# Delta-rule attention with two MLPs on one core: head-major operands, compact keys in 64x64 blocks, Newton roots, new order weights

## The chip, the cores and the metric

The kernel runs on one core of a Trainium2 chip. A core has TensorE (PE in the profile, its weight loads as PEld), VectorE (DVE), ScalarE (ACT), GpSimd (POOL) and SyncE (SP), which issues all of this kernel's DMAs; 16 DMA engines move the data. The metric is the device time of one execution in microseconds (us); less is better.

## The reference

Attention with the delta rule over 4 batches, 8 heads, 768 tokens and heads of 48, and then two gated MLPs over the 384 columns that the heads make together.

```python
k_n = k / (norm(k) + 1e-06)
for t in range(S):                       # per batch and head; state is 48x48
    y[:, :, t] = q[:, :, t] @ state
    v_old = state @ k_n[t]
    state = state + b[t] * outer(k_n[t], v[t] - v_old)
# first MLP: gate = sigmoid(causal convolution of x over 5 tokens)
x = (gate * (x @ w_val)) @ w_out
# second MLP: h = gelu(x @ w_in), halves u and v; v_n = layer norm of v
v_s = w_sg @ v_n + b_sg                  # mixes all 768 tokens of a batch
out = x + (u * v_s) @ w_out2
```

## The kernel before

**Precision.** Nearly every product is made of three float16 matmuls: an operand is split into a high and a low half, and high*high, high*low and low*high are summed (`mm3`, and `mmh` for four heads at a time). So nearly every operand is written twice: ScalarE writes the high half, VectorE or GpSimd the low one (`hl_psum`, `hl_sbuf`).

**Attention.** The 768 tokens of a batch are cut into 12 chunks of 64, 48 chunks in all (`NSEQ`). The 8 heads stand as two halves of 4: the first four in partitions 0 to 63, the others in 64 to 127, and a stationary operand is a block diagonal 128x128 matrix with zeros off the diagonal blocks, so that one matmul serves two heads. Chunks go in pairs (`d`, 24 of them), and four pairs make a set (`k`, 6 of them).

For a set, `norm(k)` loads the keys and makes reciprocal norms, with the helper `rsqrt`. For a pair, `keys(d)` scales the keys (`kf`), splits them into the block diagonal `kp` (for the first two pairs straight into `kj`), transposes them with matmuls against an identity (`pk<-i,kp`), copies the result into `kst` and lets DMAs spread it into the block diagonal; the prepared pair goes to DRAM (`keys_d`). `gram(d)` multiplies keys with keys (`pk<-kst,kp`) and takes the diagonal 32x32 blocks out into `gd` and the others into `gx`. `base(k)` inverts a set's 32x32 triangles on VectorE: 30 pairs of dependent operations (`tmp<-X` and `X<-X,tmp`) with transposes around them. `merge(d)` joins two 32-token inverses into one of 64 (`m1p`, `tbd`). `seq(n)` carries the state through the chunks: `ps_q<-wh,kj`, `rh`, `ps_q<-rh,tbd`, `wh`, `ps_state<-wh,kj`, `wh` again, each waiting for the one ahead of it. `attend(n)` makes the chunk's output from `ws`, a block diagonal copy of `wh` made by DMA, and from `qh` and `mh`. `fetch(d)` brings a prepared pair back from `keys_d` into one of two `kj` buffers.

**MLPs.** For 256 tokens at a time: `front` (convolution on VectorE, `a<-x,cw,a`), `value`, `hidden` (with a layer norm, which uses `rsqrt` on two columns), `gates`, `mix` and `final`. `mix` needs `hidden` of all of its batch's tokens, so that the last batch's mixing stands behind the last chunk of attention.

**Layout.** The attention's float16 operands have the head as their innermost index: a stationary operand of one head is read with a step of 4 elements, and so is the moving operand `wh`.

**Order.** No loop sets the order. Every call is recorded as an `Op` (all instructions therefore carry the helper's line, L106), and `in_order` plays the program through with estimated costs: on each engine the ready operation with the longest remaining chain goes next. The length of a chain is a sum over its operations, weighted per engine by the table `CHAIN` (a weight on an operation's time and a charge for going over to another engine). Each engine then runs its list strictly in this order.

Of the kernel before, what the change touches and what calls it, by code (L numbers as in the profile page):

```python
# [236 lines left out]
CHAIN = dict(tensor=(0.65, 0.064), scalar=(0.756, 0.047), vector=(2.464, 0.104), gpsimd=(0.748, 0.014), sync=(2.315, 0.036))  # L237
# [88 lines left out]
def kernel(  # L326
# [19 lines left out]
    C = 64  # L346
# [14 lines left out]
    NK, NTB, NWS, LA = 2, 2, 3, 5  # L361
# [30 lines left out]
    mhalf = const.tile([P, 1], F32, name="mhalf")  # L392
    nc.gpsimd.memset(mhalf, -0.5)
# [11 lines left out]
    def bdt(nm, i):  # L405
        if (nm, i) not in bd:
            t = const.tile([P, 4, 128, PR] if nm == "ws" else [P, 2, U, 128], F16, name=f"{nm}{i}")
            clear(nc.gpsimd, t)
            bd[nm, i] = t
        return bd[nm, i]  # L410


    kj, kprep = {}, []

    def kbd_of(keys):
        return keys[:, 0:4]

    def ktb_of(keys):
        return keys[0:EP, 4:8].rearrange("p (x i) f h -> p x i f h", x=2)
# [4 lines left out]
    for t in kj[0], kj[1], *kprep:  # L424
        clear(nc.vector, t[:, 0:4])
        clear(nc.gpsimd, t[:, 4:8])
# [94 lines left out]
    def keys(d):  # L521
# [4 lines left out]
        direct, early = d < NK, d < SETD  # L526
        both = kj[d] if direct else kprep[d % NK]
        kbd, ktb = kbd_of(both), ktb_of(both)
        (nc.vector if early else nc.gpsimd).tensor_tensor(out=kf, in0=kf, in1=rs.unsqueeze(3).to_broadcast([P, 2, PR, E]),
                                                          op=ALU.mult)  # L530
# [103 lines left out]
    def fetch(d):  # L634
# [17 lines left out]
    def queries(n):  # L652
# [7 lines left out]
        for h in range(PR):  # L660
            mm3(pq[:, h, :], (ktb[:, 0, :, h], ktb[:, 1, :, h]), (qh[:, 0, h, :], qh[:, 1, h, :]), True, True)
# [10 lines left out]
    for i in range(NWS):  # L672
        whs.append(const.tile([P, 4, C, PR], F16, name=f"wh{i}"))
# [405 lines left out]
```

## Time and profile before

| | us |
|---|---|
| median of 3 runs (781.43 to 782.82) | 781.53 |
| the profiled execution | 775.91 |
| its span, first to last instruction | 773.6 |
| PE busy in the span (8088 matmuls) | 581.0 |
| DVE busy (1402 instructions) | 592.6 |
| ACT busy (958) | 492.8 |
| POOL busy (227) | 259.9 |

The span is what the rows further down divide up; 2.3 us lie around it. The profiled execution was 5.6 us faster than the median. A matmul's end is modelled in these rows, so the distance from one start to the next says more than its duration.

### The profile page before, as it was taken

Reading aid. Unit: us, or ns where it says so; the run is one execution under the profiler, and the core shown is the slowest. Engines: PE = TensorE matmul, PEld = TensorE weight load, DVE = VectorE, ACT = ScalarE, POOL = GpSimd, SP = SyncE. Lnnn points to the kernel's source line nnn. Section 1 sums busy time; section 2 is a strip of 40 time slices with the busy share of each in tenths; the row PEclk is TensorE's granted clock in tenths of the full one; section 3 lists DMA queues with packets and bytes.
Section 4 is the critical chain, followed back from the end, with each engine's and each line's share of the span. In section 5 each row is a group of like instructions: output and inputs, shape, how many; then the busy total and the mean of one; then the engine's idle time right before and its main releaser. Section 6 shows DMA issues by size and latency. Waiting matters only on the chain.

```text
span 773.6 us, 20377 instructions
## 1 busy us (share of the span) xinstructions
PE 581.0 (75%) x8088; PEld 490.3 (63%) x8088; DVE 592.6 (77%) x1402; ACT 492.8 (64%) x958; POOL 259.9 (34%) x227
## 2 busy tenths in 40 slices
PE   0433643665656666777979999999988999989897
PEld 0321333555556554556967897898785799876786
DVE  7887787987799989997778888999975875663222
ACT  5875773899589895879646699745463644534111
POOL 7646313526543474336260154200330400011100
PEclk9999985556755577989989999999999999999999
DMA  5451623588578856728638476486545182420121
GB/s 176 136 135 44 184 73 66 131 175 228 121 178 200 233 143 130 171 61 200 144 78 172 120 188 132 99 184 141 136 116 126 31 169 71 125 69 21 48 69 42
DMA packets 211183, 97.97 MB, mean 127 GB/s; under 512 B 83088, under 2 KB 203280, under 8 KB 211088
## 3 DMA queue, kind: packets, MB, share of 16 engines
q1 hardware_dynamic: 211088, 96.67, 52.0%
q8 instruction: 64, 1.05, 0.6%
q14 instruction: 31, 0.25, 0.1%
HBM read 51.81 MB, written 23.33 MB: 97 GB/s over the span
## 4 chain that ended last, share of the span: by engine, by line
PE 31%; DVE 20%; ACT 10%; DMA 5%; issue 4%; POOL 3%; SPq 1%; ACTq 0%; DVEq 0%; POOLq 0%
PE ps_mlp L106 23%; DVE a L106 5%; PE ps_y L106 3%; DVE X L106 2%; PE ps_q L106 2%; DMA m1p<-gx 2%; DMA kj<-keys_d 2%; DVE tmp L106 2%; POOL rs L106 1%; DVE wh L106 1%; DVE ps_mlp L106 1%; PE pk L106 1%; ACT v L106 1%; DVE rs_t L106 1%; ACT tbh L106 1%
## 5 line engine op out<-in xcount | busy, mean ns | idle before, releaser
L106 PEld LDWEIGHTS <-kj 112*128 112x128 f16 (+1 forms) x1712 | 121.4, 119 | 82.1 <-issue 51.0
L106 PE MATMUL ps_mlp<-wg,vnh 128*128 128x256 f16 x864 | 141.6, 276 | 5.6 <-ACT vnh L106 3.7
L106 PEld LDWEIGHTS <-kp 112*128 112x128 f16 (+1 forms) x880 | 65.1, 122 | 49.7 <-issue 28.1
L106 PEld LDWEIGHTS <-vnh 128*128 128x128 f16 x864 | 82.9, 100 | 14.0 <-ACT vnh L106 4.5
L106 DVE SCALAR_TENSOR_TENSOR a<-x,cw,a 128x256 f32<-128x256 f32 x144 | 82.3, 607 | 0.1
L106 PEld LDWEIGHTS <-ws 112*128 112x128 f16 (+1 forms) x1104 | 74.3, 119 | 10.0 <-issue 7.6
L106 PE MATMUL ps_mlp<-gth,w 128*128 128x256 f16 x432 | 79.9, 276 | 0.1
L106 PE MATMUL ps_mlp<-gvh,wi 128*128 128x256 f16 x432 | 77.6, 280 | 1.2 <-ACT o L106 0.5
L106 DVE TENSOR_TENSOR X<-X,tmp 128x30 f32<-128x30 f32 (+9 forms) x180 | 75.9, 422 | 1.5
L106 PEld LDWEIGHTS <-m1p 128*128 128x128 f16 x1152 | 62.2, 101 | 20.0 <-issue 11.0
L106 PE MATMUL ps_state<-wh,kj 128*128 128x48 f16 x528 | 55.1, 221 | 22.3 <-DVE wh L106 12.1
L106 DVE TENSOR_TENSOR tmp<-X 128x30 f32<-128x30 f32 (+9 forms) x180 | 69.6, 387 | 1.3
L106 PE MATMUL ps_q<-wh,kj 112*128 112x48 f16 x528 | 55.4, 219 | 20.0 <-DVE wh L106 12.3
L106 PE MATMUL ps_mlp<-wi,gvh 128*128 128x512 f16 x216 | 65.8, 405 | 5.5 <-DVE gvh L106 4.8
L106 POOL TENSOR_TENSOR kp<-kf,kp 64x384 f16<-64x384 f32 x42 | 47.0, 1120 | 55.2 <-ACT kp L106 44.3
L106 PE MATMUL ps_y<-mh,ws 128*128 128x64 f16 x576 | 63.5, 208 | 1.9 <-DVE mh L106 1.9
L106 PE MATMUL ps_y<-qh,ws 112*128 112x64 f16 x528 | 61.1, 208 | 4.1 <-DVE mh L106 4.0
L106 PE MATMUL pk<-kst,kp 112*128 112x64 f16 x504 | 51.5, 236 | 13.2 <-ACT kst L106 10.1
L106 PE MATMUL ps_mlp<-gvh,wo 128*128 128x256 f16 x324 | 56.8, 273 | 4.3 <-DVE gth L106 2.8
L106 ACT ACTIVATE kst<-pk 112x512 f16<-112x512 f32 x42 | 56.5, 1345 | 3.2 <-PE pk L106 2.6
L106 PE MATMUL ps_mlp<-xh,wv 128*128 128x256 f16 x324 | 51.8, 278 | 8.4 <-POOL xh L106 6.3
L106 PE MATMUL ps_q<-rh,tbd 128*128 128x48 f16 x576 | 42.8, 195 | 16.8 <-DVE rh L106 9.0
(147 smaller groups left out, 1544.6 us busy)
## 6 DMA issues: line engine op xcount, KB each, us to landing
keys_d<-kp SPq DMA_DIRECT2D x44, 256.0 KB, 4.2
ws<-wh SPq DMA_DIRECT2D x88, 128.0 KB, 3.6
kj<-keys_d SPq DMA_DIRECT2D x44, 256.0 KB, 4.9
wg<-wgd SPq DMA_DIRECT2D x12, 768.0 KB, 5.4
qf<-in_qt SPq DMA_DIRECT2D x24, 224.0 KB, 3.4
kf<-in_kn SPq DMA_DIRECT2D x12, 384.0 KB, 4.2
vf<-in_vn SPq DMA_DIRECT2D x24, 192.0 KB, 4.9
xd<-ys SPq DMA_DIRECT2D x48, 96.0 KB, 2.5
```

Source lines behind the costliest of these rows:

```text
L106: op.call()
```

## The change

1. `ws`, `kj` and `wh` become head-major: the head stands outside, and a head's 128 (or 64, or 48) columns lie next to each other. Stationary operands are then read with step 1, and so are `wh` and `kst` as moving operands; ScalarE and VectorE write them with step 1. A DMA into a block diagonal now writes runs of 64 elements (128 bytes) where it wrote 256 (512 bytes).
2. The two block diagonal buffers `kp` and the tile `kst` go; three compact buffers `kc` hold both the split keys and their transposes. The split is one ScalarE and one GpSimd instruction over 128 partitions in place of two of each over 64. The transposing and the key-by-key matmuls of each head half are single 64x64 blocks: 32 and 48 of them for a pair of chunks in place of 16 and 24. The DMAs from `kst` into `kp` go, and a prepared pair is stored by one DMA with 4 KB for a partition in place of two.
3. `gram` takes the diagonal blocks out by one ScalarE and one VectorE instruction with a mask (`which`) in place of four ScalarE instructions over 32 partitions.
4. `rsqrt` starts from a bit trick and makes three Newton steps, all on VectorE; GpSimd's power goes. That is 11 VectorE instructions in place of 3 (and one on GpSimd), for 6 norms and 12 layer norms.
5. The `CHAIN` weights are others, so that each engine's order changes throughout.

```diff
-CHAIN = dict(tensor=(0.65, 0.064), scalar=(0.756, 0.047), vector=(2.464, 0.104), gpsimd=(0.748, 0.014), sync=(2.315, 0.036))
+CHAIN = dict(tensor=(0.304, 0.758), scalar=(0.128, 0.167), vector=(2.092, 0.053), gpsimd=(0.876, 0.428), sync=(1.949, 0.262))
...
-        kj[d] = const.tile([P, 8, 128, PR], F16, name=f"kj{d}")
-        kprep.append(const.tile([P, 8, 128, PR], F16, name=f"kp{d}"))
+        kc.append(const.tile([P, 8, PR, C], F16, name=f"kc{d}"))
...
+        kj[d] = const.tile([P, 8, PR, 128], F16, name=f"kj{d}")
...
-        nc.gpsimd.tensor_tensor(out=y, in0=x, in1=mhalf.to_broadcast([P, n]), op=ALU.pow)
-        nc.vector.scalar_tensor_tensor(out=t, in0=y, scalar=-0.5, in1=y, op0=ALU.mult, op1=ALU.mult)
-        nc.vector.tensor_tensor(out=t, in0=t, in1=x, op=ALU.mult)
-        nc.vector.scalar_tensor_tensor(out=y, in0=t, scalar=1.5, in1=y, op0=ALU.add, op1=ALU.mult)
+        ti = t.bitcast(I32)
+        nc.vector.tensor_scalar(out=ti, in0=x.bitcast(I32), scalar1=1, scalar2=None, op0=ALU.logical_shift_right)
+        nc.vector.tensor_scalar(out=y.bitcast(I32), in0=ti, scalar1=-1.0, scalar2=float(0x5F3759DF),
+                                op0=ALU.mult, op1=ALU.add)
+        for _ in range(3):
+            nc.vector.scalar_tensor_tensor(out=t, in0=y, scalar=-0.5, in1=y, op0=ALU.mult, op1=ALU.mult)
+            nc.vector.tensor_tensor(out=t, in0=t, in1=x, op=ALU.mult)
+            nc.vector.scalar_tensor_tensor(out=y, in0=t, scalar=1.5, in1=y, op0=ALU.add, op1=ALU.mult)
...
-        for r in range(2):
-            eng = nc.vector if early and r == 0 else nc.gpsimd
-            rr, ff = slice(r * C, (r + 1) * C), slice(r * C, r * C + E)
-            hi, lo = (kbd[rr, 2 * x:2 * x + 2, ff].rearrange("p i e h -> p i h e") for x in range(2))
-            nc.scalar.activation(out=hi, in_=kf[rr], func=AF.Copy)
-            eng.tensor_tensor(out=lo, in0=kf[rr], in1=hi, op=ALU.subtract)
+        nc.scalar.activation(out=hi, in_=kf, func=AF.Copy)
+        eng.tensor_tensor(out=lo, in0=kf, in1=hi, op=ALU.subtract)
...
-                nc.tensor.matmul(out=pk[:, u, :], lhsT=kbd[:, 2 * x + u // PR, :, u % PR], rhs=i64, start=True, stop=True)
+                for r in range(2):
+                    rr = slice(r * C, (r + 1) * C)
+                    nc.tensor.matmul(out=pk[rr, u, :], lhsT=both[rr, 2 * x + u // PR, u % PR, :], rhs=i64[rr], start=True,
+                                     stop=True)
...
-        to_bd(ktb.rearrange("p x i t h -> p (x i) t h"), kst.rearrange("p x i t h -> p (x i) t h"), E)
-        for r in range(0 if direct else 2):
-            rr = slice(r * C, (r + 1) * C)
-            nc.sync.dma_start(out=keys_d[d, rr], in_=both[rr, :, rr].rearrange("p x t h -> p x (t h)"))
+        if d < NK:
+            to_bd(kj[d], both)
+        else:
+            nc.sync.dma_start(out=keys_d[d], in_=both.rearrange("p x h f -> p x (h f)"))
...
-            mm3(pg[:, u, :], (ktb[:, 0, i, :, h], ktb[:, 1, i, :, h]), (kst[:, 0, i, :, h], kst[:, 1, i, :, h]), True, True)
-        for r in range(4):
-            o = 32 * (r % 2)
-            dst, src = gd[32 * r:32 * r + 32, us, :], pg[32 * r:32 * r + 32, :, o:o + 32]
-            nc.scalar.activation(out=dst, in_=src, func=AF.Copy, scale=1.0 / (SK * SK))
+            for r in range(2):
+                rr = slice(r * C, (r + 1) * C)
+                k = (kst[rr, i, h, :], kst[rr, 2 + i, h, :])
+                mm3(pg[rr, u, :], k, k, True, True)
+
+        nc.scalar.activation(out=gd, in_=pg[:, :, 0:32], func=AF.Copy, scale=which[:, 0:1])
+        nc.vector.scalar_tensor_tensor(out=gd, in0=pg[:, :, 32:64], scalar=which[:, 1:2], in1=gd, op0=ALU.mult, op1=ALU.add)
...
-            nc.sync.dma_start(out=kj[d][rr, :, rr].rearrange("p x t h -> p x (t h)"), in_=keys_d[d, rr])
+            nc.sync.dma_start(out=kj[d][rr, :, :, rr], in_=keys_d[d, rr].rearrange("p x (h f) -> p x h f", h=PR))
```

Two places in the order matter further down. The first is VectorE's list at the third set's norm (`rs_t`, `rs` and `ss` belong to `rsqrt`; `tmp` and `X` to the second set's inversion). Before:

```order
L106 SCALAR_TENSOR_TENSOR wh_101<-ps_q,wh_101 128x4x48
L106 TENSOR_TENSOR X<-X,tmp 128x4x27
L106 SCALAR_TENSOR_TENSOR rs_t<-rs 128x32
L106 SCALAR_TENSOR_TENSOR gx<-pk,gx 128x256
L106 TENSOR_TENSOR tmp<-X 128x130
L106 TENSOR_TENSOR rs_t<-rs_t,ss 128x32
```

The first `rs_t` reads GpSimd's power, with the inversion's operations queued behind it. The same place of the changed kernel:

```order
L106 TENSOR_SCALAR rs_t<-ss 128x32
L106 TENSOR_TENSOR X<-X,tmp 128x3x28
L106 TENSOR_SCALAR rs<-rs_t 128x32
L106 TENSOR_TENSOR tmp<-X 128x108
L106 SCALAR_TENSOR_TENSOR rs_t<-rs 128x32
L106 TENSOR_TENSOR X<-X,tmp 128x4x27
L106 TENSOR_TENSOR rs_t<-rs_t,ss 128x32
L106 TENSOR_TENSOR tmp<-X 128x130
L106 SCALAR_TENSOR_TENSOR rs<-rs_t,rs 128x32
```

The root now stands on VectorE alone, one step between each two of the inversion. The second place is PE's list in the changed kernel near chunk 28, where a product of keys with keys (`pk<-kc`, 64x64) falls among work on operands of 128 rows, the MLP's and the attention's:

```order
L106 LDWEIGHTS gvh
L106 MATMUL ps_mlp<-wi,gvh 128x512
L106 LDWEIGHTS tbd_94
L106 MATMUL ps_q<-rh,tbd_94 128x48
L106 LDWEIGHTS kc_89
L106 MATMUL pk<-kc_89 64x64
L106 LDWEIGHTS ws_96
L106 MATMUL ps_y<-qh,ws_96 128x64
```

In the kernel before such work alternated too (here `pk<-kst,kp` between a matmul of the MLP and one of the state), but each took the array whole:

```order
L106 LDWEIGHTS wv
L106 MATMUL ps_mlp<-xh,wv 128x256
L106 LDWEIGHTS kp_91
L106 MATMUL pk<-kst,kp_91 128x64
L106 LDWEIGHTS kj_90
L106 MATMUL ps_state<-wh_102,kj_90 128x48
```

What moved is the shape: the interleaving was there, the switching between 64x64 and the whole array was not. In the changed list the 1920 blocks of 64x64 stand in 349 stretches, of which 266 are one block alone.

## Rows read from the trace of the kernel before

**Rows 1.** Stages: length, busy us (instructions) of each engine, granted clock, DMA share, GB/s.

```profile
0.00:48.00 48.00, 12.57 (x176) 10.66 (x176) 36.43 (x66) 34.04 (x64) 30.42 (x41) 1.00 0.54 162
48.00:123.00 75.00, 34.67 (x312) 20.07 (x313) 62.65 (x144) 50.51 (x91) 28.74 (x29) 0.92 0.36 93
123.00:344.00 221.00, 137.24 (x2351) 117.23 (x2351) 196.03 (x455) 173.87 (x328) 105.70 (x84) 0.67 0.68 159
344.00:663.00 319.00, 297.69 (x4386) 260.36 (x4384) 256.65 (x643) 202.76 (x417) 84.45 (x64) 0.98 0.58 132
663.00:773.00 110.00, 98.80 (x868) 81.98 (x866) 40.81 (x98) 31.65 (x59) 10.55 (x10) 1.00 0.18 53
```

**Rows 2.** Tile wh: count, ns min/median/max, first and last start.

```profile
L106 DVE SCALAR_TENSOR_TENSOR wh<-ps_q,wh x48: 559/592/628, 122.6 to 662.1; 128x192 f16<-128x192 f32 x48
```

**Rows 3.** Timeline, DVE: start us, us, instruction; a first and a twenty-first.

```profile
47.88 1.22 DVE L106 SCALAR_TENSOR_TENSOR gd<-gd,beta_sb 128x1024 f32<-128x1024 f32 x1
...
343.86 0.58 DVE L106 SCALAR_TENSOR_TENSOR wh<-ps_q,wh 128x192 f16<-128x192 f32 x1
```

**Rows 4.** Timeline at the third norm, DVE and POOL; brackets: idle before, releaser.

```profile
122.12 5.41 POOL L106 TENSOR_TENSOR rs<-ss,mhalf 128x32 f32<-128x32 f32 x1 [1.63 <-DVE ss L106]
122.56 0.57 DVE L106 SCALAR_TENSOR_TENSOR wh<-ps_q,wh 128x192 f16<-128x192 f32 x1
122.93 0.30 DVE L106 TENSOR_TENSOR X<-X,tmp 128x108 f32<-128x108 f32 x1
127.57 0.19 DVE L106 SCALAR_TENSOR_TENSOR rs_t<-rs 128x32 f32<-128x32 f32 x1 [4.34 <-POOL rs L106]
127.68 0.43 DVE L106 SCALAR_TENSOR_TENSOR gx<-pk,gx 128x256 f16<-128x256 f32 x1
```

**Rows 5.** Waits over the span: who for whom, us in total, times, longest.

```profile
DVE rs_t L106 <- POOL rs L106: 18.2, 6, 4.5
```

**Rows 6.** Groups by shape: count, busy us, mean ns of one, idle before.

```profile
L106 ACT ACTIVATE kst<-pk 112x512 f16<-112x512 f32 x42 | 56.5, 1345 | 3.2 <-PE pk L106 2.6
L106 ACT ACTIVATE kp<-kf 64x384 f16<-64x384 f32 x44 | 47.0, 1074 | 10.4 <-DMA keys_d<-kp 7.0 <-POOL kf L106 2.7
L106 POOL TENSOR_TENSOR kp<-kf,kp 64x384 f16<-64x384 f32 x42 | 47.0, 1120 | 55.2 <-ACT kp L106 44.3 <-issue 6.6 <-PE ps_q L106 2.3
L106 ACT ACTIVATE gd<-pk 32x256 f32<-32x256 f32 x88 | 33.0, 375 | 8.6 <-PE pk L106 7.7
L106 ACT ACTIVATE wh<-ps_q 128x192 f16<-128x192 f32 x48 | 29.5, 614 | 16.2 <-PE ps_q L106 14.6 <-PE ps_b L106 1.4
L106 DVE SCALAR_TENSOR_TENSOR wh<-ps_q,wh 128x192 f16<-128x192 f32 x48 | 28.5, 594 | 5.2 <-ACT wh L106 4.7
L106 DVE SCALAR_TENSOR_TENSOR rh<-ps_q,rh 128x192 f16<-128x192 f32 x44 | 15.3, 348 | 1.4 <-ACT rh L106 0.7
L106 ACT ACTIVATE rh<-ps_q 128x192 f16<-128x192 f32 x44 | 14.5, 328 | 12.6 <-DVE ps_q L106 12.2
L106 ACT ACTIVATE gth<-ps_mlp 128x512 f16<-128x512 f32 x24 | 14.3, 598 | 20.3 <-DVE ps_mlp L106 12.8 <-PE ps_mlp L106 5.3 <-PE ps_b L106 2.2
L106 DVE SCALAR_TENSOR_TENSOR gx<-pk,gx 128x256 f16<-128x256 f32 x22 | 9.2, 416 | 2.4 <-ACT gx L106 2.3
```

**Rows 7.** Timeline, a GpSimd operation beside one of VectorE's inversion.

```profile
118.96 0.22 DVE L106 TENSOR_TENSOR tmp<-X 128x84 f32<-128x84 f32 x1
...
119.58 0.91 POOL L106 TENSOR_TENSOR w<-wst,w 128x384 f16<-128x384 f32 x1 [16.61 <-ACT w L106]
119.67 0.92 DVE L106 TENSOR_TENSOR X<-X,tmp 128x84 f32<-128x84 f32 x1
```

**Rows 8.** Timeline, PE: matmuls in a row, first start to last end.

```profile
124.22 0.55 PE L106 MATMUL ps_q<-wh,kj 112*128 112x48 f16 x8 [0.46 <-ACT wh L106]
...
476.59 0.98 PE L106 MATMUL pk<-kst,kp 112*128 112x64 f16 x13
...
480.19 0.46 PE L106 MATMUL ps_q<-rh,tbd 128*128 128x48 f16 x12
```

**Rows 9.** Page, DMA queue: packets, MB, share of 16 engines.

```profile
q1 hardware_dynamic: 211088, 96.67, 52.0%
```

**Rows 10.** Tile kj: idle before its instructions, us and times, by releaser.

```profile
  DMA kj<-keys_d: 2.7, 3
```

More of the change, by code (lines that the diff above doesn't have):

```diff
@@ L359 @@
     EP = C + E
-    NK, NTB, NWS, LA = 2, 2, 3, 5
+    NK, NKC, NTB, NWS, LA = 2, 3, 2, 3, 5
     NGV, NVN, NV = NTT + 1, NT + 2, 3
@@ L406, in bdt @@
         if (nm, i) not in bd:
-            t = const.tile([P, 4, 128, PR] if nm == "ws" else [P, 2, U, 128], F16, name=f"{nm}{i}")
+            t = const.tile([P, 4, PR, 128] if nm == "ws" else [P, 2, U, 128], F16, name=f"{nm}{i}")
             clear(nc.gpsimd, t)
@@ L410, in bdt @@
         return bd[nm, i]
-    kj, kprep = {}, []
-    def kbd_of(keys):
-        return keys[:, 0:4]
+    kj, kc = {}, []
     def ktb_of(keys):
-        return keys[0:EP, 4:8].rearrange("p (x i) f h -> p x i f h", x=2)
+        return keys[0:EP, 4:8].rearrange("p (x i) h f -> p x i h f", x=2)
+    for d in range(NKC):
+        kc.append(const.tile([P, 8, PR, C], F16, name=f"kc{d}"))
+        clear(nc.vector, kc[d][:, 0:4])
     for d in range(NK):
-        kj[d] = const.tile([P, 8, 128, PR], F16, name=f"kj{d}")
-        kprep.append(const.tile([P, 8, 128, PR], F16, name=f"kp{d}"))
-    for t in kj[0], kj[1], *kprep:
-        clear(nc.vector, t[:, 0:4])
-        clear(nc.gpsimd, t[:, 4:8])
+        kj[d] = const.tile([P, 8, PR, 128], F16, name=f"kj{d}")
+        clear(nc.vector, kj[d][:, 0:4])
+        clear(nc.gpsimd, kj[d][:, 4:8])
     nc.gpsimd.memset(cmask, 1.0)
@@ L432 @@
     nc.sync.dma_start(out=beta_sb, in_=beta_in)
+    which = const.tile([P, 2], F32, name="which")
+    nc.gpsimd.memset(which, 0.0)
+    for r in range(4):
+        nc.gpsimd.memset(which[32 * r:32 * r + 32, r % 2:r % 2 + 1], 1.0 / (SK * SK))
     for nm, n in (("tbd", NTB), ("m1p", 1), ("ws", NWS)):
@@ L525, in keys @@
         kf, rs = sets["kf"][:, cs], sets["rs"][:, cs]
[L526 to L530, printed above, removed]
-        for r in range(2):
-            eng = nc.vector if early and r == 0 else nc.gpsimd
-            rr, ff = slice(r * C, (r + 1) * C), slice(r * C, r * C + E)
-            hi, lo = (kbd[rr, 2 * x:2 * x + 2, ff].rearrange("p i e h -> p i h e") for x in range(2))
-            nc.scalar.activation(out=hi, in_=kf[rr], func=AF.Copy)
-            eng.tensor_tensor(out=lo, in0=kf[rr], in1=hi, op=ALU.subtract)
-        kst = pp.tile([EP, 2, 2, C, PR], F16, name="kst", tag="kst", bufs=2)
+        early = d < SETD
+        both = kc[d % NKC]
+        hi, lo = (both[:, 2 * x:2 * x + 2, :, 0:E] for x in range(2))
+        eng = nc.vector if early else nc.gpsimd
+        eng.tensor_tensor(out=kf, in0=kf, in1=rs.unsqueeze(3).to_broadcast([P, 2, PR, E]), op=ALU.mult)
+        nc.scalar.activation(out=hi, in_=kf, func=AF.Copy)
+        eng.tensor_tensor(out=lo, in0=kf, in1=hi, op=ALU.subtract)
         for x in range(2):
@@ L540, in keys @@
             for u in range(U):
-                nc.tensor.matmul(out=pk[:, u, :], lhsT=kbd[:, 2 * x + u // PR, :, u % PR], rhs=i64, start=True, stop=True)
-            pk = pk[0:EP].rearrange("p (i h) t -> p i h t", h=PR)
-            kt = kst[:, x].rearrange("p i t h -> p i h t")
+                for r in range(2):
+                    rr = slice(r * C, (r + 1) * C)
+                    nc.tensor.matmul(out=pk[rr, u, :], lhsT=both[rr, 2 * x + u // PR, u % PR, :], rhs=i64[rr], start=True,
+                                     stop=True)
+            pk = pk.rearrange("p (i h) t -> p i h t", h=PR)
+            kt = both[:, 4 + 2 * x:6 + 2 * x]
             if early and x == 1:
@@ L547, in keys @@
                 nc.scalar.activation(out=kt, in_=pk, func=AF.Copy, scale=-1.0)
-        to_bd(ktb.rearrange("p x i t h -> p (x i) t h"), kst.rearrange("p x i t h -> p (x i) t h"), E)
-        for r in range(0 if direct else 2):
-            rr = slice(r * C, (r + 1) * C)
-            nc.sync.dma_start(out=keys_d[d, rr], in_=both[rr, :, rr].rearrange("p x t h -> p x (t h)"))
-        sets["kt", d] = (ktb, kst)
+        if d < NK:
+            to_bd(kj[d], both)
+        else:
+            nc.sync.dma_start(out=keys_d[d], in_=both.rearrange("p x h f -> p x (h f)"))
     def gram(d):
         us = slice(d % SETD * U, (d % SETD + 1) * U)
-        ktb, kst = sets.pop(("kt", d))
-        gd = sets["gd"]
+        kst = kc[d % NKC][:, 4:8]
+        gd = sets["gd"][:, us, :]
         pg = bank_of(d, 2)
@@ L672 @@
     for i in range(NWS):
-        whs.append(const.tile([P, 4, C, PR], F16, name=f"wh{i}"))
+        whs.append(const.tile([P, 4, PR, C], F16, name=f"wh{i}"))
         clear(nc.gpsimd, whs[i])
```

22 lines of the change are left out of this document (10 added, 12 removed).

## The prediction

> **What bounds the kernel now.** First the busy time by stage. Up to 344 us VectorE is the fullest engine, 295 of 344 us, ScalarE follows with 258, and PE has 184, at a granted clock of 0.67, so partly at 1.2 and partly at 2.4 GHz, from 123 to 344 us. From 344 to 663 us PE is busy for 298 of 319 us at 0.98, and from 663 us on for 99 of 110 [rows 1]. The reader is to see two kernels in one: VectorE, with ScalarE feeding it, sets the pace of the first half, PE that of the second. Next where the cuts lie: the first inversion starts at 47.9 us, chunk 0 has its `wh` at 123 us, chunk 20 at 344, chunk 47 at 663 [rows 2, 3]. The tail after that is MLP work that needs the last chunk, so its length stays, and the end moves by what the two halves move. Last the waits: VectorE, in the stage that it bounds, stands still for GpSimd's power (4.34 us at the third norm, the inversion queued behind) [rows 4], 18.2 us in six norms [rows 5].
>
> **Roots.** The power takes 5.41 us [rows 4], and `rs_t` waits at the head of VectorE's list. It goes, with a wait of 18.2/6, or 3.0 us, for each norm. Four of the six norms lie before 344 us: -12 us. In its place stand 8 more VectorE operations. Such an operation lasts 0.19 us and lets the next one start after 0.11 [rows 4]; the order puts them between the inversion's steps, so I take 0.11, with 0.19 as the other end. Four norms and, by 344 us, three layer norms have 7 x 8 = 56: +6 us (to +11).
>
> **Layout on VectorE and ScalarE.** `wh` is written with a step of 4 in 0.594 us on VectorE and 0.614 on ScalarE; `rh`, of the same size with step 1, takes 0.348 and 0.328 [rows 6]. By 344 us there are 41 writes of `wh` on each: 41 x 0.246 = -10 us for VectorE, 41 x 0.286 = -12 for ScalarE. `kst` takes 1.345 us, and `gth`, as large and with step 1, 0.598: 33 instances by then, -25 us on ScalarE. The split takes ScalarE 1.074 us twice for a pair of chunks; one instruction of 384 columns lies between `rh` (192 columns, 0.328) and `gth` (512, 0.598), say 0.5: for 20 pairs -33 us. GpSimd's 1.12 us twice becomes about 0.9 once [rows 6, 7].
>
> **Mask.** Four ScalarE instructions of 0.375 us become one; with a column of scales I put it at 0.5, for some 18 pairs -18 us. VectorE gets one more, priced by `gx` (0.416, same shape): 18 x 0.42 = +7.5 us [rows 6].
>
> **Sum to 344 us.** VectorE by itself: -12 + 6 - 10 + 7.5 = -8.5 us. ScalarE loses 88 of 258 us, a third. What that is worth is the unknown: VectorE is idle for 49 of the 344 us, 12 of them counted above, so between 0 and 37 us. I take a third, -12, since a third of ScalarE's work goes; the first inversion waits for `keys` and `gram` and starts earlier within this term. GpSimd's operations hold up VectorE's: beside a POOL operation of 0.91 us, 84 columns of the inversion took 0.92 in place of 0.22 [rows 7], 0.7 us for a hit. By 344 us GpSimd has some 18 fewer of these; if half hit, -6 (0 to -12). Together -26.5 us; with every term at its good end -57, at its bad end (Newton steps at 0.19 us, no relief) -3.5.
>
> **PE, 344 to 663 us.** Eight `ps_q<-wh,kj` in a row took 0.55 us, twelve `ps_q<-rh,tbd` 0.46 [rows 8]. Taking 0.2 us off for the last one's own length leaves 50 and 24 ns from start to start. Both move 48 columns; the first reads both operands with a step of 4, the second with step 1. Some 600 such matmuls lie in this stage (25 chunks with 24 each): at 22 ns each -13 us, and since PE is 93% busy, -12. The key products took 62 ns by the same working (13 in 0.98 us). About 250 of these and of the transpositions become 450 blocks of 64x64. No row shows one; between 24 and 62 ns apiece they come to 11 to 28 us, against some 13 now: -2 to +15. I take 0, near the lower end, because a step of 1 is what the 24 ns have in common with them. Switching between shapes is a rival below. ScalarE and VectorE also lose work here, but they aren't the bound.
>
> **DMA.** Two DMAs for each pair (`kst` into `kp`) go, and `gram` no longer waits for them; a stored pair is one DMA in place of two. Against that, `ws` and fetched keys are written in runs of 128 bytes: some 190,000 such pieces replace some 80,000 of 512. The mean packet now costs 52.0% x 16 x 773.6 us / 211,088 = 30 ns of one engine [rows 9]. A piece of 128 bytes costs between a quarter of that (by bytes) and all of it, which gives from -60 to +210 us on each of 16 engines over the whole attention, now 58 to 68% occupied [rows 1]. A fetch of 128 in place of 32 pieces on each engine lands 0 to 2.9 us later. PE has waited 2.7 us in all for fetches [rows 10], since they go out a pair ahead. I count 0. The rows show 512-byte runs alone on these paths, hence both ends. The Trainium skill (DMA: Bandwidth & Descriptors, Specifications) speaks against this part: it wants 512 bytes or more for full rate and has smaller transfers read and write back; by that rule the upper end would hold, and no row of these tiles shows it yet.
>
> **Tail and order.** Three layer norms at the end trade a short power for eight small steps, +1 us. The new weights leave the pace nearly as it was: the MLP matmuls issued before chunk 20 and before chunk 47 differ by a few, and the work after chunk 47 is as large. 0 us.
>
> **Sum.** -26.5 - 12 + 1 = -37.5 from the profiled execution's 775.9 us: 738.4. That execution lay 5.6 us under the median, so 744 us as a median. With every term at its good end it would be 711, at its bad end 782.
>
> **Rivals.**
> - *Switches of the array's shape (slower).* The order has 349 stretches of 64x64 blocks, mostly one block between whole-array matmuls, 188 of them from chunk 20 on, where PE is the bound. If PE must empty before each change of shape, a matmul's 0.2 us no longer overlaps with the next one's start after 0.02: up to 0.18 us, 2 x 188 times, 68 us, of which 93% count. That gives 744 + 63 = 807 us. It decides from 0.1 us per switch on, where it eats the 38 us. For it: nothing in the trace ever changed shape, so nothing bounds it. Against: the order alternated freely at 24 to 62 ns. The Trainium skill (TensorEngine Tiling (Array Packing), Tiling Modes, Key Properties) has this very rule: changing the tiling mode, unlike changing the tile, drains TensorE. No row here can show it.
> - *VectorE stays full.* ScalarE's and GpSimd's relief buys nothing, and the Newton steps cost 0.19 us each: -12 + 11 - 10 + 7.5 = -3.5 us in the first half, with -12 and +1 after: 767 us.
> - *Short DMA pieces come late (no gain, or slower).* If all 22 fetches were late by 2.9 us with PE waiting, +64 us; half of it gives 776, all of it 808.
> - *ScalarE's relief is worth all the idle time.* -25 us more: 719.
>
> **How the numbers follow.** Forecast 0.53, switches 0.17, VectorE full 0.15, DMA 0.07, full relief 0.08. Two median values of this kernel closer than 0.2% (1.6 us) can't be told apart. Faster: 0.53 + 0.15 + 0.08, and a little of the DMA case, 0.77. Slower: 0.17 and most of the DMA case, less the switches cheap enough to leave some gain: 0.19. Same: 0.04. The range, 712 to 790, takes in the forecast's bounds, both faster rivals and the cheap half of both slow ones; some 0.15 is left out, nearly all of it above.
>
> **What would show it.** Right: `kst`-like copies near 0.6 us, `wh` near 0.35 on both engines, no VectorE wait for a power, chunk 20 some 26 us earlier and chunk 47 some 38, the tail as long as now. The switches are refuted if single 64x64 blocks between whole-array matmuls start 60 ns or less after the one ahead. Wrong: PE's busy time above 600 us with starts 150 ns apart around `kc`; chunk 20 at the same time (then VectorE's list, not its feeders, was the bound); or `ps_y` and `ps_q` waiting for DMAs into `kj` and `ws`.

## The result: 1.0% slower

The changed kernel takes 787.8 us (median of 16; 784.6 to 793.8, and one slow execution of 800.2 that the ratio leaves out) where the kernel before takes 780.0: a ratio of 1.010, 95% interval 1.007 to 1.013. The forecast was 744 us and faster; the time lies inside the range, near its upper end, and on the other side of no change, where the first rival led. The profiled execution took 793.8 us, span 792.1. That is 6 us over the median, and the profiled execution of the kernel before lay 4 us under its own (780.0), so the stages below stand 18 us apart where the medians stand 8.

The stages of the changed kernel, cut as in [rows 1] (length, busy us and instructions of each engine, granted clock, DMA share, GB/s):

```profile
0.00:48.00 48.00, 13.41 (x347) 11.75 (x348) 43.97 (x119) 26.24 (x58) 20.04 (x39) 1.00 0.65 183
48.00:123.00 75.00, 45.94 (x705) 29.06 (x705) 69.03 (x173) 38.17 (x87) 24.82 (x29) 0.78 0.40 106
123.00:344.00 221.00, 168.59 (x2717) 131.49 (x2716) 178.26 (x485) 121.96 (x288) 70.84 (x63) 0.64 0.66 141
344.00:663.00 319.00, 303.00 (x4174) 238.66 (x4174) 234.29 (x660) 156.40 (x356) 62.08 (x48) 0.93 0.58 122
663.00:792.00 129.00, 116.25 (x1109) 96.10 (x1106) 52.66 (x141) 38.05 (x75) 10.09 (x8) 0.98 0.21 60
```

VectorE is fuller up to 123 us (113 us, before 99) and emptier from 123 to 344 (178, before 196), and there TensorE is busy for 31 us more, at a granted clock of 0.64, again partly at 1.2 and partly at 2.4 GHz. Over the span PE is busy for 647 us, before for 581. VectorE's emptier stretch has waits for TensorE in it: up to 344 us `ps_y` and `ps_q` make it wait 14.5 us, in the kernel before 0.8.

```profile
DVE ps_y L106 <- PE ps_y L106: 7.9, 9, 3.2
...
DVE ps_q L106 <- PE ps_q L106: 6.6, 5, 1.9
```

The marks of [rows 3] in the changed kernel, on VectorE's timeline: first inversion, chunks 0, 16, 20 and 47.

```profile
32.97 1.33 DVE L106 SCALAR_TENSOR_TENSOR gd<-gd,beta_sb 128x1024 f32<-128x1024 f32 x1
...
107.61 0.35 DVE L106 SCALAR_TENSOR_TENSOR wh<-ps_q,wh 128x192 f16<-128x192 f32 x1
...
268.63 0.35 DVE L106 SCALAR_TENSOR_TENSOR wh<-ps_q,wh 128x192 f16<-128x192 f32 x1
...
335.54 0.36 DVE L106 SCALAR_TENSOR_TENSOR wh<-ps_q,wh 128x192 f16<-128x192 f32 x1
...
675.24 0.36 DVE L106 SCALAR_TENSOR_TENSOR wh<-ps_q,wh 128x192 f16<-128x192 f32 x1 [0.25 <-ACT wh L106]
```

Chunk 16 of the kernel before:

```profile
294.59 0.57 DVE L106 SCALAR_TENSOR_TENSOR wh<-ps_q,wh 128x192 f16<-128x192 f32 x1
```

So the first inversion and chunk 0 are 15 us ahead, chunk 16 is 26 us ahead, which is the lead that the prediction wanted by chunk 20; at chunk 20 it has shrunk to 8 us, and chunk 47 is 13 us late [rows 2]. The order has 349 stretches, that is runs of 64x64 blocks with whole-array matmuls on both sides; between chunks 16 and 20 stand 72 of them. What one of them looks like, on PE's timeline in a later such place (start us, us, instruction, count):

```profile
405.93 0.21 PE L106 MATMUL pk<-kc 64*64 64x64 f16 x1
406.07 0.19 PE L106 MATMUL ps_b<-tbh,m1p 128*128 128x32 f16 x1
406.19 0.21 PE L106 MATMUL pk<-kc 64*64 64x64 f16 x1
406.34 0.19 PE L106 MATMUL ps_b<-tbh,m1p 128*128 128x32 f16 x1
406.46 0.21 PE L106 MATMUL pk<-kc 64*64 64x64 f16 x1
```

A block starts 0.12 us after the whole-array matmul, and the next of these 0.145 us after the block: 0.265 us for the two, twelve times in a row here, where twelve whole-array `ps_q<-rh,tbd` started 24 ns apart [rows 8]. The granted clock is 1.00 here, that is 2.4 GHz. Over the whole trace, at that clock and with no idle time between, the median is 0.127 us in and 0.146 out (176 and 179 changes). The prediction held this rival refuted by starts of 60 ns or less; they are twice that, both ways, and its sign of being wrong, PE busy above 600 us with starts 150 ns apart around `kc`, is there.

Where the granted clock is 0.50, or 1.2 GHz, the two take 0.34 us:

```profile
130.31 0.26 PE L106 MATMUL pk<-i,kc 64*64 64x64 f16 x1
130.50 0.22 PE L106 MATMUL ps_q<-wh,kj 112*128 112x48 f16 x1
130.65 0.26 PE L106 MATMUL pk<-i,kc 64*64 64x64 f16 x1
```

The durations by shape came out as forecast (count; ns min, median, max; first and last start us):

```profile
L106 ACT ACTIVATE wh<-ps_q x48: 303/331/374, 105.7 to 674.9; 128x192 f16<-128x192 f32 x48
L106 DVE SCALAR_TENSOR_TENSOR wh<-ps_q,wh x48: 306/354/359, 107.6 to 675.2; 128x192 f16<-128x192 f32 x48
...
L106 ACT ACTIVATE kc<-pk x42: 570/597/621, 18.0 to 479.4; 128x512 f16<-128x512 f32 x42
...
L106 ACT ACTIVATE kc<-kf x24: 506/516/574, 15.9 to 428.3; 128x384 f16<-128x384 f32 x24
...
L106 ACT ACTIVATE gd<-pk,which x22: 450/474/478, 23.9 to 497.8; 128x256 f32<-128x256 f32 x22
```

Against [rows 6], `wh` fell from about 0.6 to 0.33 and 0.35 us, the stored keys from 1.345 to 0.597, the split from twice 1.07 to once 0.516, the diagonals from four times 0.375 to once 0.474. No VectorE wait for a power is left.

### The profile page after: what moved, and what is told of

The parts are those of the page before. It is cut to its first block, busy times and chain, and to the rows that moved or that the text cites. A ratio compares the mean times of both kernels' runs of the same rounds, so it can differ in the third digit from the quotient of the medians.

```text
span 792.1 us, 22147 instructions
## 1 busy us (share of the span) xinstructions
PE 647.2 (82%) x9048; PEld 507.1 (64%) x9048; DVE 578.2 (73%) x1571; ACT 380.8 (48%) x862; POOL 187.9 (24%) x187
## 2 busy tenths in 40 slices
DMA packets 327638, 94.41 MB, mean 119 GB/s; under 512 B 274544, under 2 KB 316912, under 8 KB 327536
## 3 DMA queue, kind: packets, MB, share of 16 engines
q1 hardware_dynamic: 327536, 93.00, 52.4%
## 4 chain that ended last, share of the span: by engine, by line
PE 49%; DVE 35%; ACT 5%; issue 4%; DMA 4%; SPq 1%; ACTq 0%; DVEq 0%
PE ps_mlp L106 28%; PE pk L106 8%; PE ps_y L106 6%; DVE a L106 6%; DVE X L106 4%; DVE tmp L106 4%; PE ps_q L106 3%; DVE wst L106 2%; PE ps_b L106 2%; PE ps_state L106 2%; DVE ps_mlp L106 2%; DVE gd L106 2%; DVE wh L106 1%; DVE st L106 1%; DVE m1p L106 1%
## 5 line engine op out<-in xcount | busy, mean ns | idle before, releaser
L106 PEld LDWEIGHTS <-kc 64*64 64x64 f16 x1920 | 78.2, 134 | 79.6 <-issue 31.8
L106 PEld LDWEIGHTS <-kj 112*128 112x128 f16 (+1 forms) x1632 | 92.7, 104 | 45.0 <-issue 30.4
L106 PE MATMUL pk<-i,kc 64*64 64x64 f16 x704 | 53.6, 231 | 26.3 <-ACT kc L106 20.6
L106 PE MATMUL pk<-kc 64*64 64x64 f16 x1056 | 64.6, 223 | 10.2 <-ACT kc L106 4.6
L106 PEld LDWEIGHTS <-ws 112*128 112x128 f16 (+1 forms) x1104 | 55.3, 107 | 17.9 <-issue 11.3
L106 PE MATMUL ps_mlp<-gth,w 128*128 128x256 f16 x432 | 63.7, 273 | 1.6 <-DVE gth L106 0.9
L106 PE MATMUL ps_mlp<-xh,wv 128*128 128x256 f16 x324 | 58.4, 300 | 6.6 <-DVE gvh L106 2.5
L106 PE MATMUL ps_mlp<-gvh,wi 128*128 128x256 f16 x432 | 63.0, 275 | 0.9 <-ACT o L106 0.5
L106 POOL TENSOR_TENSOR vnh<-v,vnh 128x512 f16<-128x512 f32 x24 | 28.4, 1196 | 118.5 <-ACT vnh L106 118.5
L106 DVE SCALAR_TENSOR_TENSOR ps_mlp<-ps_mlp,gl,bs 128x256 f32<-128x256 f32 x48 | 22.7, 488 | 43.1 <-PE ps_mlp L106 42.9
L106 PE MATMUL ps_state<-wh,kj 128*128 128x48 f16 x528 | 40.4, 195 | 13.0 <-DVE wh L106 10.3
```

Source lines behind the costliest of these rows:

```text
L106: op.call()
```

## The experiments

Three theories at the start. **S**: each change between 64x64 blocks and whole-array matmuls holds TensorE. **M**: the blocks are dear by their number. **W**: the new chain weights, or the Newton roots, put the work in a worse order. Each ratio is against the kernel before, timed beside it; the letters of later theories are those of the expectations.

**The same work with the blocks together.** Only the planner's choice among ready matmuls is changed (the rest of the order follows from it):

```diff
                 op = heappop(now[e])[2]
+                if e == "tensor":
+                    if block(last.get(e)) and not block(op):
+                        more = [q for q in now[e] if block(q[2])]
+                        if more:
+                            heappush(now[e], (-op.chain, op.index, op))
+                            now[e].remove(min(more))
+                            heapify(now[e])
+                            op = min(more)[2]
+                    last[e] = op
...
+def block(op):
+    return op is not None and op.kw["lhsT"].shape[0] == 64
```

> Same work as the changed kernel; the planner alone is changed: once it has put a 64x64 block on TensorE it takes the next ready 64x64 block before any whole-array matmul, so the 1920 blocks stand in 54 stretches where the changed kernel has 349 (16 from chunk 20 on, where it has 181). Theory S (each change between 64x64 blocks and whole-array matmuls holds TensorE about 0.1 us, 0.2 us for going over and back): 165 stretches less from chunk 20 on at 0.2 us are 33 us, those ahead of it give up to 15 more, so 740 to 757 us, with chunk 47 at 630 to 645 us and PE busy below 600 us. Theory M (the blocks are dear by their number, 1920 in place of 960 matmuls, wherever they stand): within 5 us of 788. Theory W (the new chain weights put the work in a worse order): within 8 us of 788.

Measured: 717.9 us, 0.920 (0.916 to 0.923), 70 us below the changed kernel, more than S asked for (740 to 757), and far from M and W. Its stages up to 663 us, its marks of chunks 20 and 47, and its blocks:

```profile
0.00:48.00 48.00, 13.41 (x347) 11.75 (x348) 43.60 (x117) 25.98 (x57) 20.00 (x39) 1.00 0.65 183
48.00:123.00 75.00, 44.96 (x753) 29.08 (x753) 71.60 (x180) 40.94 (x93) 26.62 (x31) 0.78 0.39 104
123.00:344.00 221.00, 150.71 (x3099) 126.89 (x3097) 205.52 (x545) 139.40 (x320) 83.50 (x72) 0.73 0.78 166
344.00:663.00 319.00, 297.58 (x4453) 249.59 (x4449) 251.93 (x709) 166.73 (x377) 59.42 (x45) 1.00 0.57 119
```

```profile
312.27 0.36 DVE L106 SCALAR_TENSOR_TENSOR wh<-ps_q,wh 128x192 f16<-128x192 f32 x1
...
600.56 0.36 DVE L106 SCALAR_TENSOR_TENSOR wh<-ps_q,wh 128x192 f16<-128x192 f32 x1 [0.25 <-ACT wh L106]
```

```profile
366.56 0.44 PE L106 MATMUL pk<-i,kc 64*64 64x64 f16 x16
...
372.27 0.95 PE L106 MATMUL pk<-kc 64*64 64x64 f16 x48
```

Sixteen blocks take 0.44 us and 48 take 0.95; less 0.2 us for the last one's own length that is 16 ns from start to start, at 2.4 GHz. From chunk 20 to 47 the grouped kernel takes 288 us and the changed one 340. Of these 51 us, 165 stretches fewer at 0.265 less 0.05 us (two starts without a change) explain 35; the granted clock from 344 to 663 us, 2.4 GHz throughout here and 0.93 of it with the stretches in between, goes the same way and may hold the rest, which no run separates. The other 23 us were lost ahead of chunk 20, 19 of them by chunk 16, which the grouped kernel reaches at 249.7 us. Marks alone mislead here, because the planner also moves MLP matmuls across them: from chunk 16 to 20 the changed kernel takes 67 us with 101 MLP matmuls, and the grouped one 63 us, but with 160. The grouped kernel with four diagonals (further down) has 99 of them and 8 stretches there, and takes 50 us. That points to the stretches for the lead that was lost between these chunks.

**More stretches, by the old weights.**

```diff
-CHAIN = dict(tensor=(0.304, 0.758), scalar=(0.128, 0.167), vector=(2.092, 0.053), gpsimd=(0.876, 0.428), sync=(1.949, 0.262))
+CHAIN = dict(tensor=(0.65, 0.064), scalar=(0.756, 0.047), vector=(2.464, 0.104), gpsimd=(0.748, 0.014), sync=(2.315, 0.036))
```

> The changed kernel with the CHAIN weights of the kernel before. Its order has 507 stretches of 64x64 blocks in place of 349, 282 in place of 181 from chunk 20 on. Theory S: 101 stretches more at 0.2 us are 20 us, so 800 to 815 us. Theory M: 780 to 796 us. Theory W: faster than the changed kernel, 755 to 775 us.

Measured: 842.7 us, 1.081 (1.076 to 1.087). W falls, since undoing the weights costs 55 us; S has the direction but was too low (800 to 815).

**More stretches, by the opposite rule.** Against the grouped kernel:

```diff
-                    if block(last.get(e)) and not block(op):
-                        more = [q for q in now[e] if block(q[2])]
+                    if block(last.get(e)) and block(op):
+                        more = [q for q in now[e] if not block(q[2])]
```

> The opposite of the grouped order: after a 64x64 block the planner takes a ready whole-array matmul first, so the same 1920 blocks stand in 777 stretches (371 from chunk 20 on, 190 more than the changed kernel). Theory S: 190 x 0.2 us are 38 us, the 238 more stretches ahead of chunk 20 some 10 to 30 us, so 820 to 860 us. Theory M and theory W: 780 to 800 us, the work and the weights are those of the changed kernel.

Measured: 926.0 us, 1.187 (1.183 to 1.191). With the same 1920 blocks, 54, 349, 507 and 777 stretches give 718, 788, 843 and 926 us: 0.24 us for each stretch between the first two, 0.32 between the second and the last. S was too low again (820 to 860). The single gaps account for 0.22 at 2.4 GHz (0.265 less two starts of 25 ns) and for 0.26 at 1.2 GHz (0.34 less two starts of 40 ns), and the slower clock has a larger share where the stretches are many: from chunk 20 to 47 the granted clock is 0.99, 0.93, 0.85 and 0.83 in the four. What else makes a stretch dear is not shown: the third kernel has other weights, and every one has its own order.

**No 64x64 blocks at all.** The old preparation, head-major (two of its places; the old buffers and their DMAs come back with it):

```diff
-                    nc.tensor.matmul(out=pk[rr, u, :], lhsT=both[rr, 2 * x + u // PR, u % PR, :], rhs=i64[rr], start=True,
-                                     stop=True)
+                nc.tensor.matmul(out=pk[:, u, :], lhsT=kbd[:, 2 * x + u // PR, u % PR], rhs=i64, start=True, stop=True)
...
-                mm3(pg[rr, u, :], k, k, True, True)
+            mm3(pg[:, u, :], (ktb[:, 0, i, h], ktb[:, 1, i, h]), (kst[:, 0, i, h], kst[:, 1, i, h]), True, True)
```

> The changed kernel with the key preparation of the kernel before (block-diagonal kp and kj, 960 matmuls of the whole array, kst and its two DMAs, two hi and two lo operations a set), head-major like the rest; masked diagonals, Newton roots and new weights stay. Theory S: no change of shape is left on TensorE, ScalarE and GpSimd have the old load of about 9 us more, so 740 to 765 us. Theory M: 740 to 765 us too, 960 matmuls less. Theory W, or one that blames the Newton roots: 775 to 795 us.

Measured: 751.2 us, 0.963 (0.959 to 0.967). It fits S; with the grouped run M is out, since the grouped kernel has all 1920 blocks and is 33 us faster than this one.

**Which part of the shape counts.** The whole-array kernel with its 384 transpositions cut by columns (first diff, for both halves `rr`), then by rows (second; this one leaves out the keys of the second half):

```diff
-                nc.tensor.matmul(out=pk[:, u, :], lhsT=kbd[:, 2 * x + u // PR, u % PR], rhs=i64, start=True, stop=True)
+                    nc.tensor.matmul(out=pk[rr, u, :], lhsT=kbd[:, 2 * x + u // PR, u % PR, rr], rhs=i64, start=True, stop=True)
```

```diff
-                nc.tensor.matmul(out=pk[:, u, :], lhsT=kbd[:, 2 * x + u // PR, u % PR], rhs=i64, start=True, stop=True)
+                nc.tensor.matmul(out=pk[:, u, :], lhsT=kbd[0:C, 2 * x + u // PR, u % PR], rhs=i64[0:C], start=True, stop=True)
```

> The whole-array kernel of the earlier run (751.2 us) with the 384 transpositions of keys split by columns: 768 matmuls of 128 rows and 64 columns, in 125 stretches. Where a transposition of whole shape followed another matmul there it started 40 ns after it (median), and the next one 52 ns after the last. Theory C (a change in the columns of a tile holds TensorE as a change to 64x64 does): some 120 to 150 ns in and 145 to 190 ns out, and 125 x 0.28 = 35 us more, so 775 to 795 us. Theory R (only the rows count): 60 ns or less both ways, and 745 to 760 us.

> The whole-array kernel of the earlier run with the 384 transpositions of keys on 64 rows and all 128 columns (the keys of the second half of the rows are left out), in 65 stretches. Theory R (a change in the rows of a tile holds TensorE): 120 to 150 ns in and 145 to 190 ns out, 13 more stretches than there were of the whole shape and 65 now with a price, so 755 to 775 us. Theory C (only the columns count): 60 ns or less both ways, and 745 to 757 us.

Measured, with one execution each: 768.3 us for columns and 747.1 for rows. Both are lower than the theories that held had asked (775 to 795, 755 to 775), and the time for rows is the one that theory C gave (745 to 757), no longer than that of the whole-array kernel. So the times don't settle it; the gaps decide. PE's timeline by columns, by rows, and in the whole-array kernel:

```profile
412.27 0.20 PE L106 MATMUL ps_q<-rh,tbd 128*128 128x48 f16 x1
412.39 0.22 PE L106 MATMUL pk<-i,kp 128*64 128x64 f16 x1
412.54 0.20 PE L106 MATMUL ps_q<-rh,tbd 128*128 128x48 f16 x1
```

```profile
422.17 0.20 PE L106 MATMUL ps_state<-wh,kj 128*128 128x48 f16 x1
422.30 0.20 PE L106 MATMUL pk<-i,kp 64*128 64x64 f16 x1
422.43 0.20 PE L106 MATMUL ps_state<-wh,kj 128*128 128x48 f16 x1
```

```profile
432.47 0.25 PE L106 MATMUL ps_y<-mh,ws 128*128 128x64 f16 x3
432.56 0.25 PE L106 MATMUL ps_y<-qh,ws 112*128 112x64 f16 x3
432.65 0.25 PE L106 MATMUL ps_y<-mh,ws 128*128 128x64 f16 x3
```

0.12 in and 0.15 out for the columns, 0.13 and 0.13 for the rows; over the two traces the median way out at 2.4 GHz is 0.149 us (65 times) and 0.132 (34). Either is enough to hold TensorE, so what C and R say of the gaps holds for both. That a change of rows costs time in the end was not shown. A change from 128 to 112 rows costs nothing: three matmuls each in 0.09 us.

**The parts one by one.** Newton roots in the kernel before (`rsqrt` of the change alone); head-major operands alone, for `ws`, `kj`, `kp`, `kst` and `wh` alike; both:

```diff
-            t = const.tile([P, 4, 128, PR] if nm == "ws" else [P, 2, U, 128], F16, name=f"{nm}{i}")
+            t = const.tile([P, 4, PR, 128] if nm == "ws" else [P, 2, U, 128], F16, name=f"{nm}{i}")
```

> The kernel before with the Newton roots and nothing else of the change. The prediction's terms of this part are 12 us of VectorE waits and 6 us of port time against 6 us of added operations: 12 us net, so 768 to 776 us. Rival (the old load of ScalarE holds VectorE anyway, so that the wait moves to ScalarE): 777 to 786 us.

> The kernel before with head-major operands and nothing else of the change: old key preparation on the whole array, power roots, four diagonal operations, old weights. The prediction's terms of this part alone are 12 us off TensorE after 344 us, 10 us off VectorE and about a third of 37 us off ScalarE ahead of it, so 745 to 755 us if they hold. If the DMA pieces of 128 bytes cost what the layout gives: 775 us or more. If the layout is worth more than the prediction said: below 740 us.

> Head-major operands and Newton roots, without the 64x64 blocks, the mask and the new weights. Theory I (each part alone is held back by what the other takes away: GpSimd's roots kept VectorE waiting 23 us ahead of 344 us where the layout stood alone): more than the two gains together, 745 to 757 us. Theory A (the parts add up): the kernel before less 10 us of the layout less the gain of the Newton roots alone, 758 to 768 us.

Measured: Newton 764.3 us, 0.980 (0.973 to 0.987), 16 us; layout 774.1, 0.989 (0.982 to 0.996), 9 us; both 758.5, 0.974 (0.968 to 0.981), 20 us. The parts add up within the intervals, theory I falls, and the layout is worth a third of what it was priced at. Then the grouped kernel with single parts undone: power roots (first diff), the old weights (as above), four diagonal operations (second diff).

```diff
...
-        for _ in range(3):
...
+        nc.gpsimd.tensor_tensor(out=y, in0=x, in1=mhalf.to_broadcast([P, n]), op=ALU.pow)
...
```

```diff
-        nc.scalar.activation(out=gd, in_=pg[:, :, 0:32], func=AF.Copy, scale=which[:, 0:1])
...
+            nc.scalar.activation(out=dst, in_=src, func=AF.Copy, scale=1.0 / (SK * SK))
```

> The grouped order (717.9 us, 54 stretches) with the square roots of the kernel before: GpSimd's power and one Newton step on VectorE (56 stretches). Theory N (the roots were worth what the prediction said, 12 us of VectorE waits and some port time against 6 us of added operations): 723 to 733 us, with waits of VectorE for rs of 8 to 20 us. Rival (VectorE is less of a bound now and the three Newton steps cost it what the waits did): 712 to 721 us.

> The grouped order with the CHAIN weights of the kernel before (55 stretches). Theory A (once the stretches are grouped, the weights move nothing that matters, as the prediction had it): 712 to 726 us. Theory B (the new weights by themselves gave part of the gain that the prediction missed): 730 us or more.

> The grouped order with the four diagonal operations on ScalarE in place of the masked pair (57 stretches). By the prediction's terms the mask takes 18 us off ScalarE and puts 7.5 us on VectorE. Theory A (a wash on VectorE, which bounds the stretch up to about 320 us): 712 to 724 us. Theory B (ScalarE's relief reaches VectorE): 725 to 735 us without the mask.

Measured: 744.0 us with the power, 0.950 (0.944 to 0.957), so Newton is worth 24 us here, more than either theory gave it (723 to 733 at most); VectorE waits again:

```profile
DVE rs_t L106 <- POOL rs L106: 23.5, 6, 5.1
```

With the old weights 729.1 us, 0.931 (0.926 to 0.936): between the two theories, 9 us by ratio. With four diagonals 715.9 us, 0.914 (0.909 to 0.919), as fast as with the mask within the intervals: theory A.

**Why the layout gives so little, and the compact preparation so much.** The layout alone changes the DMA queue and brings waits of PE for DMAs. In the kernel before, [rows 10] has 2.7 us for `kj`, and PE has no wait for `ws` at all. Page and waits of the layout-alone kernel:

```profile
q1 hardware_dynamic: 444560, 96.67, 67.6%
...
PE ps_y L106 <- DMA ws<-wh: 13.2, 8, 4.7
...
PE ps_q L106 <- DMA kj<-keys_d: 7.3, 1, 7.3
```

The loss lies ahead of chunk 20: that mark comes at 357.1 us, 13 later than before, and the stage from there to chunk 47 takes 300 us, 18 less.

Theory D: its 128-byte pieces. Three quarters of the keys' DMA (the store below and the fetch likewise) are left out of the whole-array kernel, of the layout alone, and of the kernel before as a control:

```diff
-            nc.sync.dma_start(out=keys_d[d, rr].rearrange("p x (h f) -> p x h f", h=PR), in_=both[rr, :, :, rr])
+            nc.sync.dma_start(out=keys_d[d, rr].rearrange("p x (h f) -> p x h f", h=PR)[:, 0:2], in_=both[rr, 0:2, :, rr])
```

> The whole-array kernel (751.2 us, DMA engines busy 65.6%) with three quarters of each set's DMA into keys_d and back into kj left out (2 of 8 blocks are moved; the rest of kj keeps what stood there). Theory D (the 128-byte pieces are what holds the layout to 10 us and the whole-array kernel 33 us above the grouped one): 725 to 740 us. Rival P (it is the operations of the old preparation and its longer way, not the pieces): 747 to 754 us, with the DMA share down all the same.

> Head-major operands alone (774.1 us, DMA engines busy 67.6%) with the same three quarters of the DMA of keys_d and kj left out. Theory D: the layout then gives what the prediction said of it, 750 to 762 us. Rival P: 769 to 777 us.

> The control for the two light kernels: the kernel before, its pieces of 256 bytes as they were, with the same three quarters of the DMA of keys_d and kj left out. Theory D (it is the 128-byte pieces that hold the layout): the kernel before gains little, 772 to 782 us, where the head-major one gained 31 us. Rival V (any DMA less gives that much, whatever its pieces): 750 to 762 us.

Measured: 728.0 us, 0.929 (0.924 to 0.933), from 0.963; 743.1, 0.947 (0.941 to 0.954), from 0.989; the control 783.5, 1.003 (1.000 to 1.005). The layout alone came out faster than theory D asked (750 to 762), and the control lies just above what D gave it (772 to 782). (The pieces of the control are of 512 bytes; the 256 in its expectation is a slip.) The same volume is free in long pieces and costs 32 us in short ones. Then the opposite, on the grouped kernel: two DMAs more for each pair of chunks, in short pieces and in long rows.

```diff
+        to_bd(spare[d % 2], both)
```

```diff
+            nc.sync.dma_start(out=spare[d % 2][rr], in_=both[rr].rearrange("p x h f -> p x (h f)"))
```

> The grouped kernel (717.9 us) with two DMAs a set more, that write each set of prepared keys in 128-byte pieces into a spare tensor that nobody reads: about 2050 pieces a set, as many as the old preparation had more. Theory D: 725 to 745 us. Rival P: 715 to 722 us.

> The control for the heavy kernel (748.8 us): the grouped kernel with two DMAs a set more of the same bytes into a spare tensor, in rows of 2 KB and not in pieces of 128 bytes. Theory D: 717 to 726 us. Rival V (two more issues a set on the queue, or the bytes, cost it): 738 to 752 us.

Measured: 748.8 us, 0.955 (0.950 to 0.960), against 0.920, above what theory D gave; and 734.1, 0.939 (0.935 to 0.942), between the two theories. (The short pieces were 4,096 packets a pair; the expectation counted one DMA of the two. The long rows were of 4 KB; the 2 in the expectation is a slip.) Here V and D share it: the volume and the issues cost 1.9%, the pieces 1.6% more. That suggests less room on the queue of the grouped kernel (58.4% of the span) than on that of the kernel before (52.0%), though here DMAs were added and there taken away. That the compact preparation is worth 34 us over the old one (0.963 to 0.920) fits the DMA that it saves (444,560 packets to 327,536); its fewer operations weren't priced apart.

**Fewer or cheaper stretches still.** The planner adds the price of a change:

```diff
+                    if block(last.get(e)) != block(op):
+                        t += 0.12
```

> The grouped kernel with a planner that also adds 0.12 us to TensorE's time at each change of tile shape (60 stretches, 14 from chunk 20 on). Theory S leaves it little: 705 to 722 us. Anything above 725 would say that the planner's times elsewhere matter more than the stretches.

Measured: 709.6 us, 0.904 (0.901 to 0.907), the fastest kernel here, with six stretches more than the grouped one (from chunk 20 on two fewer); so what it gains is not their number, and the truer times for TensorE that the planner then has are the likely reason, not a tested one.

## Why the prediction was wrong, step by step

- **Switches of shape: the step that failed.** The prediction named the mechanism, put its break-even at 0.1 us for each switch, and left it out of the sum with a chance of 0.17, because the order "alternated freely at 24 to 62 ns". But all those matmuls took the array whole (112 or 128 rows, 128 columns); that is no evidence on a change of shape. Measured: 0.12 us in, 0.145 out, or 0.11 us for each switch beyond a plain start, just above the break-even; 70 us in all with 295 stretches more (718 to 788). From chunk 20 on the trace has 180 stretches, not the 188 of the prediction. The Trainium skill (TensorEngine Tiling (Array Packing), Tiling Modes, Key Properties) says that a change of tiling mode drains TensorE, and the traces agree as far as starts of 0.12 and 0.145 us in place of 24 ns can show it. The rival's 807 us was too high because the rest of the change gave 62 us, not 38.
- **First half.** -26.5 us by chunk 20. Grouped: 312.3 against 343.9, -32. Right in size, in part by luck: no run has its terms one by one, and the layout alone put chunk 20 13 us later. In the changed kernel 26 us stood at chunk 16 and 8 at chunk 20.
- **Roots.** -12 for the waits, +6 for the steps, -6 for GpSimd's hold-ups: -12. Measured alone 16 us, with chunk 20 11 us earlier (332.6): right. In the grouped kernel it is 24, of which chunk 20 shows 8 (319.9 against 312.3); why it is worth more there stays open.
- **Mask.** A third of 18 us against 7.5: about nothing, and the run without it shows no difference beyond the intervals. Right.
- **TensorE from chunk 20 to 47.** -12 us, measured 318 to 288, -30: mis-sized. The 22 ns for each of 600 matmuls held (`ps_q<-wh,kj` starts 47 ns apart in the kernel before and 25 in the grouped one, medians at 2.4 GHz; [rows 8] alone would have given 26 ns). The blocks, counted at a net 0, cost 16 ns apiece when together, below the lower end of 24, which makes 430 of them some 6 us cheaper than what they replace, an estimate. Another 4 us are not a gain: 40 of the stage's 1589 MLP matmuls, at 109 ns apiece, stand in other stages of the grouped kernel. And the weight loads weren't counted: with head-major operands they are shorter too, and may hold the rest, which no run separates. Kernel before, then grouped (count, busy us, mean ns, idle before):

```profile
L106 PEld LDWEIGHTS <-kj 112*128 112x128 f16 (+1 forms) x1712 | 121.4, 119 | 82.1 <-issue 51.0
```

```profile
L106 PEld LDWEIGHTS <-kj 112*128 112x128 f16 (+1 forms) x1632 | 84.8, 103 | 43.5 <-issue 33.2
```

- **DMA, counted at 0.** For the whole change that held: the changed kernel has 327,536 packets at 52.4% of the span, where [rows 9] has 52.0%, and `ps_y` waits 0.5 us for `ws`. It held by a cancellation: the layout's pieces cost 32 us, and the compact preparation takes some 117,000 of the 444,560 packets away, and with them nearly all of `ps_y`'s 13.2 us of waits for `ws`. No run took pieces out of the changed or the grouped kernel, so what the remaining ones cost stays open. A piece is nearer to the lower end: from the kernel before to the layout alone, busy time grows by 1,915 us of one engine; if some 78,000 runs of 512 bytes became four pieces each, a piece takes 14 ns where a run took 30, an estimate from the two pages. The packets themselves bear it out: those of 128 bytes took 14.3 ns each in the layout alone, those of 512 took 34.1 in the kernel before (means). The upper end is not what the time shows, though by the byte a piece does cost 1.7 to 1.9 times as much. The Trainium skill (DMA: Bandwidth & Descriptors, Specifications) has pieces under 512 bytes read and written back; by that rule the prediction let a piece cost as much as a run of 512, and 14.3 ns are less than half of 34.1.
- **New weights, counted at 0.** They are worth 9 us with the blocks together and 55 in the changed kernel, where they give 349 stretches in place of 507; 158 stretches at 0.24 to 0.32 us are 38 to 51. Comparing how many MLP matmuls go out by chunk 20 didn't show that.
- **Tail.** +1 us; 117 us from chunk 47 to the end, before 112: a little more than forecast.
- **Rivals.** VectorE full: refuted, since the first half gave 32 us with the blocks together where that rival had 3.5. Full relief: its 719 us is the grouped kernel's 718, but by luck, since it put 51 us into the first half, which gave 32. What holds of it is that VectorE is busy for 321 of 344 us in the grouped kernel and idle for 23 in place of 49. Late DMA: by the waits not in the change as a whole, but in the layout alone.

## What to carry to other kernels

Before a matmul is cut into smaller tiles, count how often the order goes from one tile shape to another, not how many matmuls there are: here 349 stretches in place of 54 ate a gain of 62 us and 8 more, and one rule in the planner that keeps the blocks together turned 1% slower into 8% faster. A layout that suits the engines can cost on the DMA queues what it gives, so price its pieces as a part of it. And a rival with a known mechanism that nothing in the trace excludes deserves more than the chance of a mishap.

## What was not expected of the hardware

A change of the tile's rows alone, or of its columns alone, holds TensorE as a change of both does (0.13 and 0.13, 0.12 and 0.15 us), while 112 and 128 rows mix freely at 30 ns. Blocks of 64x64 that follow each other start 16 ns apart at 2.4 GHz, closer than whole-array matmuls of 48 columns at 24. And the granted clock was lower where the stretches were many: from chunk 20 to 47 it was 0.99 with 54 of them, 0.93 with 349 and 0.83 with 777. The stretches don't set it alone, since it was 0.98 in the kernel before, which has none, and 0.96 in the grouped kernel with the old weights, which has 55.
